# RWKV mixing and a PReLU feed-forward on one core: tiles moved to other addresses, and the last three steps' output products in another order

## The chip, the cores and the metric

One core of a Trainium2 chip runs the whole kernel. The metric is device microseconds of one execution. The kernel before has a median of 498.93 us over three runs (497.51, 498.93, 500.3). One further execution was profiled; everything read from a trace below is from it.

## The reference, cut to what matters

A recurrent mixing layer writes its output `x`, and a feed-forward with a leaky rectifier follows. All is float32.

```
for t in range(768):                       # batch 4, heads 8, head size 48
    cur   = (u * k[t]) outer v[t]
    y[t]  = r[t] @ (state + cur)
    state = w * state + k[t] outer v[t]
x = y as [3072 tokens, 384]
h = x @ w_in                               # 384 x 2048
g = max(h, 0) + alpha * min(h, 0)
out = g @ w_out                            # 2048 x 384
```

## The kernel before, in words

The sequence is cut into 6 chunks of 128 positions. With 4 batches a chunk is 512 tokens. The mixing layer of a chunk is done in a chunked form by small float32 products, in "bursts", one for each of 4 pairs of heads (function `burst`, lines 543 to 605). Their moving operands are slices of 64 columns of `raw` and `base` and of 48 columns of `v`.

The feed-forward (called MoE in the change) takes a chunk in 16 steps of 128 hidden units, 96 steps in all. To keep float32 precision every operand is split into a rounded part and a rest: weights into `wh` and `wl`, the input into `xh` and `xl`, the hidden values into `gh` and `gl`. A product is then three matmuls: high by high, low by high, high by low.

- `m_in(n)`, line 628: nine matmuls of 128x128 weights with 512 moving columns make `h` of one step in one bank of PSUM, three blocks `k` of the contraction by three products. The moving tiles are `xh` and `xl`.
- Then ScalarE copies `h` to `g` (line 636), VectorE makes the rectifier (637), ScalarE rounds it to `gh` (640) and VectorE subtracts to get `gl` (641). `gl` is written by line 641 alone.
- `m_out(n)`, line 661: nine matmuls add the step's share to the three sums `acc0`, `acc1`, `acc2` (one for each block of 128 output rows). The moving tiles are `gh` (six matmuls) and `gl` (three). In every step but the last the order is product by product: `gh` with `wh` into the three sums, `gh` with `wl`, `gl` with `wh`. In the last step it is sum by sum.
- After a chunk's last step ScalarE copies each sum to SBUF (line 688) and a DMA on SyncE's queue stores it (line 690).

`m_out` runs three steps behind `m_in` (`MLAG = 3`), so that the three outer products that are left come one behind the other at the end. The order of all work is planned ahead: each piece has an engine, an estimate of its time, what it reads and writes, and a rank; a list scheduler places a piece as soon as it can begin, the lowest rank first. The result is written out in that order with the scheduling layer in manual mode; that layer adds the semaphore waits from what it sees of tiles and banks.

Tiles have fixed addresses. They are placed one behind the other, each padded to a multiple of 32 bytes. First come the constants and weights (`wh`, `wl`), then the pool `wk`, whose tiles stand in the order in which their names are first used. Small tiles of an odd number of 32-byte units put all that follows off a multiple of 64.

Of the kernel before, what the change touches and what calls it, by code (L numbers as in the profile page):

```python
# [9 lines left out]
F32R = mybir.dt.float32r  # L10
# [14 lines left out]
MLAG = 3  # L25
# [151 lines left out]
def rwkv_prelu_kernel(ctx: ExitStack, tc, rk, vkr, wP, uP, u, wall, alpha, w, r_all, k_all, v_all, oT):  # L177
# [19 lines left out]
    def fixed(shape, name, dt=F32):  # L197
        t = const.tile(shape, dt, name=name)
        return plan.buf(lambda: t)
# [14 lines left out]
    T = [None] * P  # L214

    uw = fixed([112, P, 2], "uw")
    wh, wl = ([fixed([128, 2 * NK, 128], f"{n}{i}", F32R) for i in range(NF)] for n in ("wh", "wl"))
    flag = fixed([1, 1], "flag", I32)

    bank = pb([128, NT], "acc2")  # L220
    plan.banks += [ps.tile([128, NT], F32, name=f"bank{i}") for i in range(5)]
# [256 lines left out]
            cu(), sums()[:, cols].rearrange("p (b g) -> p g b", g=2), AF.Copy), r=[mine], w=[cu], rank=copy_rank)  # L478


    seen_y = fixed([1, 2], "seen_y")
    pairs = [(c, q) for c in range(1, C) for q in range(P)]
    made = {}

# [39 lines left out]
    def burst(i, was, at):  # L524
# [28 lines left out]
        if before:  # L553
            (c0, q0), r0, v0, base0, *states0 = before
            y = [psum() for _ in range(2)]
            uses += [r0, v0, base0, *states0]
            spare = psum()
            writes += y

            def where(g, b, j):  # L560
                o = g ^ (b >> 1)
                return y[g]()[half(o), (b & 1) * L + j * HI:(b & 1) * L + (j + 1) * HI]

            def through_state():
                for j, t in enumerate(states0):
                    for e in range(2):
                        for g in range(2):
                            for b in (e, e + 2):
                                nc.tensor.matmul(where(g, b, j), t()[half(g), b],  # L569
                                                 r0()[half(g), b, HI * j:HI * (j + 1)], start=(j == 0 and e == 0),  # L570
                                                 stop=False, skip_group_check=True)

            def through_scores(crossed):
                for e in (1, 0) if crossed else (0, 1):
                    for g in (1, 0) if crossed else (0, 1):
                        j = g ^ crossed
# [71 lines left out]
    def m_out(n):  # L648
# [11 lines left out]
            for k in ks:  # L660
                nc.tensor.matmul(banks[k](), a[i]()[:, NK + k], x(), start=(begin and j == 0), stop=(end and j == 2))  # L661

        if n == NM - 1:
            for k in range(NK):
                add("PE", 0.7, lambda k=k: [mm(j, (k,)) for j in range(3)], r=[wh[i], wl[i], gh, gl], w=[banks[k]],
                    rank=n + MLAG - 0.5)
        else:
            for j in range(3):
                add("PE", 0.7, lambda j=j: mm(j, range(NK)), r=[wh[i], wl[i], gl if j == 2 else gh], w=banks,
                    rank=n + MLAG - 0.5)  # L670
        if end:
            again = c in seen
            seen.add(c)
            for k in range(NK):
# [19 lines left out]

    def check():

        ok, w2, total = sb([128, NF + P], "ok", 1), sb([112, P], "w2", 1), sb([1, 1], "total", 1)
        count = psum()
        at = 40
        add("POOL", 0.1, lambda: nc.gpsimd.memset(ok(), 0.0), w=[ok], rank=at)  # L700
        add("DVE", 0.1, lambda: nc.vector.tensor_scalar(ok()[:, 0:NF], alph(), 1.0, None, op0=ALU.is_le), r=[alph],
            w=[ok], rank=at)
        add("DVE", 0.1, lambda: nc.vector.tensor_tensor(out=w2(), in0=wp(), in1=wp(), op=ALU.mult), r=[wp], w=[w2],
            rank=at)
        add("DVE", 0.1, lambda: nc.vector.tensor_scalar(ok()[0:112, NF:], w2(), 0.75 ** 2, None, op0=ALU.is_ge),
            r=[w2], w=[ok], rank=at)
        add("DVE", 0.1, lambda: nc.vector.scalar_tensor_tensor(
            out=ok()[0:112, NF:], in0=w2(), scalar=0.75 ** -2, in1=ok()[0:112, NF:], op0=ALU.is_le, op1=ALU.mult),
            r=[w2], w=[ok], rank=at)
        add("PE", 0.3, lambda: nc.tensor.matmul(count()[0:1, 0:NF + P], one()[:, 0:1], ok(), start=True, stop=True), r=[one, ok],  # L710
            w=[count], rank=at)
        add("DVE", 0.1, lambda: nc.vector.tensor_reduce(out=total(), in_=count()[0:1, 0:NF + P], axis=AX.X, op=ALU.add), r=[count],
            w=[total], rank=at)
        add("DVE", 0.1, lambda: nc.vector.tensor_scalar(total(), total(), DFF + 112 * P - 0.5, None, op0=ALU.is_lt),
            w=[total], rank=at)
        add("DVE", 0.1, lambda: nc.vector.tensor_copy(flag(), total()), r=[total], w=[flag], rank=at)


    def warm():
# [180 lines left out]
```

## Time and profile before

| what | value |
|---|---|
| median of three runs | 498.93 us |
| the profiled execution's own time | 498.5 us |
| its span, first to last instruction | 496.7 us |
| TensorE (PE) busy | 477.7 us, 96% |
| VectorE (DVE) busy | 322.1 us, 65% |
| ScalarE (ACT) busy | 242.5 us, 49% |
| DMA, mean over the span | 95 GB/s |

The execution takes 1.8 us more than its span. PE is busy nearly throughout; its matmuls overlap in the records, so that the pace is read from the starts of successive matmuls and from the chain of waits, and not from the busy time of one. A row `L661 PE MATMUL acc<-gl,wh` is a matmul of line 661 that reads `gl` as moving and `wh` as weights and writes a sum.

### The profile page before, as it was taken

The page shows a single profiled execution, that of the slowest core. Times are in us where ns is not written, and L with a number is a line of the kernel's source. Part 1 is how long each engine was busy: PE and PEld are TensorE (multiplying, and loading weights), DVE is VectorE, ACT ScalarE, POOL GpSimd, SP SyncE. Part 2 cuts the span into 40 slices and gives each one's busy share as a digit, 9 for nine tenths or more (in the row PEclk, how much of TensorE's full clock was granted, in tenths as well). Part 3 has the DMA queues.
Part 4 walks back from the last instruction along what each step waited for, and adds up shares of the span by engine and source line. Part 5 has one row for each costly group of instructions (what it writes and reads, how often), then busy time and mean ns, then how long its engine had stood idle before and what let it go on. Part 6 is the DMA issues. An engine that isn't in the chain of part 4 may idle for free.

```text
span 496.7 us, 11103 instructions
## 1 busy us (share of the span) xinstructions
PE 477.7 (96%) x4563; PEld 390.2 (79%) x4563; DVE 322.1 (65%) x550; ACT 242.5 (49%) x565; POOL 45.1 (9%) x49
## 2 busy tenths in 40 slices
PE   7989878999999999999999999999999999999994
PEld 6857756788888888888888888888888878888883
DVE  7799999999986677656647546747535434333331
ACT  3777557666764455535535635535633333423332
POOL 2000100001312112100311101211000000000000
PEclk9799999999999999999999999999999999999998
DMA  7965575374152253413212213312120000100001
GB/s 220 299 172 189 153 226 196 126 233 161 49 189 90 80 169 100 147 43 83 86 36 86 95 56 84 86 36 70 63 54 1 1 1 1 64 0 2 0 1 68
DMA packets 24888, 47.39 MB, mean 95 GB/s; under 512 B 4096, under 2 KB 12416, under 8 KB 24832
## 3 DMA queue, kind: packets, MB, share of 16 engines
q1 hardware_dynamic: 24832, 46.62, 30.3%
q8 instruction: 38, 0.62, 0.5%
q14 instruction: 18, 0.15, 0.1%
HBM read 37.96 MB, written 6.29 MB: 89 GB/s over the span
## 4 chain that ended last, share of the span: by engine, by line
PE 84%; DVE 8%; ACT 3%; DMA 2%; issue 1%; SPq 0%; DVEq 0%; ACTq 0%
PE acc L661 38%; PE bank L628 36%; PE bank L569 2%; PE bank L579 2%; PE bank L550 2%; PE bank L543 2%; DMA wraw<-wall 1%; DVE wx L333 1%; DVE xl L362 1%; DMA raw<-rk 1%; DVE wl L337 1%; DVE wx L330 1%; DVE g L637 1%; PE acc L473 1%; DVE raw L496 1%
## 5 line engine op out<-in xcount | busy, mean ns | idle before, releaser
L637 DVE SCALAR_TENSOR_TENSOR g<-bank,alph,g 128x512 f32<-128x512 f32 x96 | 72.0, 750 | 110.0 <-ACT g L636 108.5
L636 ACT ACTIVATE g<-bank 128x512 f32<-128x512 f32 x96 | 57.3, 597 | 141.0 <-PE bank L628 139.1
L628 PE MATMUL bank<-xh,wh 128*128 128x512 f32 x288 | 113.6, 395 | 3.4 <-DVE T L605 3.4
L628 PE MATMUL bank<-xh,wl 128*128 128x512 f32 x288 | 112.3, 390 | 0.4 <-DVE wl L337 0.3
L628 PE MATMUL bank<-xl,wh 128*128 128x512 f32 x288 | 112.1, 389 | 0.0
L640 ACT ACTIVATE gh<-g 128x512 fp32r<-128x512 f32 x96 | 60.6, 632 | 71.3 <-DVE g L637 71.1
L641 DVE TENSOR_TENSOR gl<-g,gh 128x512 fp32r<-128x512 f32 x96 | 70.0, 730 | 37.1 <-ACT gh L640 37.0
L661 PE MATMUL acc<-gh,wh 128*128 128x512 f32 x288 | 83.6, 397 | 1.6 <-ACT gh L640 1.6
L661 PE MATMUL acc<-gl,wh 128*128 128x512 f32 x288 | 83.2, 396 | 0.0
L661 PE MATMUL acc<-gh,wl 128*128 128x512 f32 x288 | 81.7, 391 | 0.0
L628 PEld LDWEIGHTS bank<-xh,wh 128*128 128x128 f32 x288 | 54.1, 188 | 15.8 <-ACT wx L326 3.8
L628 PEld LDWEIGHTS bank<-xh,wl 128*128 128x128 f32 x288 | 54.1, 188 | 12.6 <-DVE wl L337 1.3
L661 PEld LDWEIGHTS acc<-gl,wh 128*128 128x128 f32 x288 | 54.1, 188 | 12.1
L628 PEld LDWEIGHTS bank<-xl,wh 128*128 128x128 f32 x288 | 54.0, 188 | 11.7
L661 PEld LDWEIGHTS acc<-gh,wl 128*128 128x128 f32 x288 | 53.9, 188 | 11.6
L661 PEld LDWEIGHTS acc<-gh,wh 128*128 128x128 f32 x288 | 52.6, 188 | 13.2 <-ACT gh L640 1.9
L507 POOL TENSOR_TENSOR rr<-rr,kk 128x384 f32<-128x384 f32 x16 | 21.4, 1337 | 294.9 <-DMA kk<-vkr 155.8
L518 ACT ACTIVATE base<-ident,cu 128x64 f32<-128x64 f32 x160 | 41.4, 337 | 1.1 <-DVE cu L513 1.0
L362 DVE TENSOR_TENSOR xl<-bank,xh 48x256 fp32r<-48x256 f32 (+2 forms) x85 | 37.2, 438 | 3.5 <-ACT xh L361 1.7
L361 ACT ACTIVATE xh<-bank 48x256 fp32r<-48x256 f32 (+2 forms) x85 | 33.3, 392 | 7.8 <-PE bank L431 3.4
L496 DVE TENSOR_TENSOR raw<-raw,W 112x512 f32<-112x512 f32 x40 | 26.3, 681 | 0.3 <-DMA raw<-rk 0.3
L509 POOL TENSOR_TENSOR rr<-rr,utab 128x384 f32<-128x384 f32 x16 | 21.0, 1310 | 1.3
(93 smaller groups left out, 375.1 us busy)
## 6 DMA issues: line engine op xcount, KB each, us to landing
wraw<-wall SPq DMA_DIRECT2D x16, 768.0 KB, 4.8
raw<-rk SPq DMA_DIRECT2D x46, 224.0 KB, 4.2
v<-vkr SPq DMA_DIRECT2D x24, 192.0 KB, 4.0
kk<-vkr SPq DMA_DIRECT2D x24, 192.0 KB, 3.6
rr<-vkr SPq DMA_DIRECT2D x16, 192.0 KB, 2.4
oT<-o SPq DMA_DIRECT2D x12, 256.0 KB, 2.1
oT<-g SPq DMA_DIRECT2D x6, 256.0 KB, 2.6
xh<-xh SPq DMA_DIRECT2D x36, 32.0 KB, 2.5
```

Source lines behind the costliest of these rows:

```text
L361: add("ACT", us, lambda: nc.scalar.activation(to(h), view(), AF.Copy), r=[src], w=refs(h), rank=rank)
L362: add("DVE", us + 0.1, lambda: nc.vector.tensor_tensor(out=to(l), in0=view(), in1=to(h), op=ALU.subtract), r=[src] + refs(h), w=refs(l), r ...
L496: add("DVE", 0.72, lambda t=t, tab=tab: nc.vector.tensor_tensor(out=t().rearrange("p b (j t) -> p (b j) t", j=2), in0=t().rearrange("p b ( ...
L507: add("POOL", 1.2, lambda: nc.gpsimd.tensor_tensor(out=rt(), in0=rt(), in1=k(), op=ALU.mult), r=[k] + ([wh[12]] if c == 2 else []), w=[rt] ...
L509: add("POOL", 1.2, lambda: nc.gpsimd.tensor_tensor(out=rt().rearrange("p (g b) e -> p g b e", g=2), in0=rt().rearrange("p (g b) e -> p g b ...
L518: add("ACT", 0.32, lambda g=g, b=b: nc.scalar.activation(base()[:, g, b], ident2(), AF.Copy, scale=cu()[:, g, b:b + 1]), r=[cu, ident2], w ...
L628: nc.tensor.matmul(hp()[:, :], a[i]()[:, k], x[c]()[:, k], start=(k == 0 and j == 0), stop=(k == NK - 1 and j == 2))
L636: add("ACT", 0.6, lambda: nc.scalar.activation(g(), hp()[:, :], AF.Copy), r=[hp], w=[g], rank=n - 100)
L637: add("DVE", 0.75, lambda: nc.vector.scalar_tensor_tensor(out=g(), in0=hp()[:, :], scalar=alph()[:, i:i + 1], in1=g(), op0=ALU.mult, op1=A ...
L640: add("ACT", 0.64, lambda: nc.scalar.activation(gh(), g(), AF.Copy), r=[g], w=[gh], rank=n - 100)
L641: add("DVE", 0.73, lambda: nc.vector.tensor_tensor(out=gl(), in0=g(), in1=gh(), op=ALU.subtract), r=[g, gh], w=[gl], rank=n - 99)
L661: nc.tensor.matmul(banks[k](), a[i]()[:, NK + k], x(), start=(begin and j == 0), stop=(end and j == 2))
```

## The change

Three things.

Addresses. `flag` and `seen_y`, 32 bytes each, now stand between `wh` and `wl` in place of behind `wl`; the tile `ok` grows from 80 to 128 bytes a partition, `w2` and `total` to 64. By the addresses in the two built programs, `gl`, `base`, `v`, `o` and `wraw` began 32 bytes past a multiple of 64 before (`gl` at 168864, 170912 and 172960), and begin at multiples of 64 now (168896, 170944, 172992). `xh`, `xl` and `gh` began at multiples of 64 before too; they are 64 bytes further on now, as is `wl`. `raw` and the three work tiles `g` stay where they were.

Order. The outer products of the last three steps (numbers 93, 94, 95) are pieces of one sum each, with ranks that put the first two sums ahead of the third. On PE the last rows stand so; `acc_4946`, `acc_4948` and `acc_4950` are the three sums, and the number behind `wh` or `wl` tells the step's weights (the kernel before first):

```order
2802 L661 MATMUL acc_4946<-gl,wh_95 128x512 [waits DVE_49]
2803 L661 MATMUL acc_4948<-gl,wh_95 128x512
2804 L661 MATMUL acc_4950<-gl,wh_95 128x512
2805 L661 MATMUL acc_4946<-gh,wh_96 128x512 [waits Activation_49]
2806 L661 MATMUL acc_4946<-gh,wl_112 128x512
2807 L661 MATMUL acc_4946<-gl,wh_96 128x512 [waits DVE_49]
2808 L661 MATMUL acc_4948<-gh,wh_96 128x512
2809 L661 MATMUL acc_4948<-gh,wl_112 128x512
2810 L661 MATMUL acc_4948<-gl,wh_96 128x512
2811 L661 MATMUL acc_4950<-gh,wh_96 128x512
2812 L661 MATMUL acc_4950<-gh,wl_112 128x512
2813 L661 MATMUL acc_4950<-gl,wh_96 128x512
```

The changed kernel at the same place of PE:

```order
2802 L660 MATMUL acc_4946<-gh,wh_96 128x512 [waits Activation_49]
2803 L660 MATMUL acc_4946<-gh,wl_114 128x512
2804 L660 MATMUL acc_4946<-gl,wh_96 128x512 [waits DVE_49]
2805 L660 MATMUL acc_4948<-gh,wh_96 128x512
2806 L660 MATMUL acc_4948<-gh,wl_114 128x512
2807 L660 MATMUL acc_4948<-gl,wh_96 128x512
2808 L660 MATMUL acc_4950<-gh,wh_95 128x512
2809 L660 MATMUL acc_4950<-gh,wl_113 128x512
2810 L660 MATMUL acc_4950<-gl,wh_95 128x512
2811 L660 MATMUL acc_4950<-gh,wh_96 128x512
2812 L660 MATMUL acc_4950<-gh,wl_114 128x512
2813 L660 MATMUL acc_4950<-gl,wh_96 128x512
```

The first sum is ready with the 18th of the last 27 matmuls (before with the 21st), the second with the 21st (before the 24th), the third with the 27th as before. The last step's `gl` is first read by the 18th (before by the 21st). Ahead of these 27 matmuls, PE's instructions stand in the same order in both kernels, and so do those of the other engines.

The last copy. The third sum goes to SBUF in two halves of 256 columns: ScalarE the first, VectorE the second. The end of ScalarE's and of VectorE's queue, the kernel before (ScalarE, then VectorE; the last rows ahead of the test of `flag`):

```order
416 L640 ACTIVATE gh<-g 128x512 [waits DVE_49]
417 L688 ACTIVATE o<-acc_4946 128x512 [waits DMAHW4_49,PE_49]
418 L688 ACTIVATE o<-acc_4948 128x512 [waits DMAHW5_49,PE_49]
419 L688 ACTIVATE g<-acc_4950 128x512 [waits PE_49,Activation_49]
...
549 L637 SCALAR_TENSOR_TENSOR g<-bank_115,alph,g 128x512 [waits Activation_49]
550 L641 TENSOR_TENSOR gl<-g,gh 128x512 [waits PE_49,Activation_49]
```

And the changed kernel:

```order
416 L639 ACTIVATE gh<-g 128x512 [waits DVE_49]
417 L694 ACTIVATE o<-acc_4946 128x512 [waits DMAHW4_49,PE_49]
418 L694 ACTIVATE o<-acc_4948 128x512 [waits DMAHW5_49,PE_49]
419 L689 ACTIVATE g<-acc_4950 128x256 [waits PE_49,Activation_49]
...
549 L636 SCALAR_TENSOR_TENSOR g<-bank_116,alph,g 128x512 [waits Activation_49]
550 L640 TENSOR_TENSOR gl<-g,gh 128x512 [waits PE_49,Activation_49]
551 L691 COPY g<-acc_4950 128x256 [waits Activation_49]
```

VectorE's copy waits for a count of ScalarE's semaphore and for none of PE's. The store of the third sum, which waited for ScalarE, waits for VectorE now.

The diff, cut to its core:

```diff
-    wh, wl = ([fixed([128, 2 * NK, 128], f"{n}{i}", F32R) for i in range(NF)] for n in ("wh", "wl"))
-    flag = fixed([1, 1], "flag", I32)
+    wh = [fixed([128, 2 * NK, 128], f"wh{i}", F32R) for i in range(NF)]
+    flag, seen_y = fixed([1, 1], "flag", I32), fixed([1, 2], "seen_y")
+    wl = [fixed([128, 2 * NK, 128], f"wl{i}", F32R) for i in range(NF)]
...
-        if n == NM - 1:
+        if n >= NM - 3:
+
             for k in range(NK):
+                late = n == NM - 1 or k == NK - 1
                 add("PE", 0.7, lambda k=k: [mm(j, (k,)) for j in range(3)], r=[wh[i], wl[i], gh, gl], w=[banks[k]],
-                    rank=n + MLAG - 0.5)
+                    rank=NM + (k == NK - 1) + 0.5 * late + 0.1 * k + 0.01 * (n - NM))
...
+                elif n == NM - 1 and k == NK - 1:
+                    add("ACT", 0.4, lambda o=o, t=banks[k]: nc.scalar.activation(
+                        o()[:, 0:256], t()[:, 0:256], AF.Copy), r=[banks[k]], w=[(o, 0)], rank=n - 90)
+                    add("DVE", 0.4, lambda o=o, t=banks[k]: nc.vector.tensor_copy(
+                        o()[:, 256:512], t()[:, 256:512]), r=[banks[k]], w=[(o, 1)], rank=n - 90)
...
-        ok, w2, total = sb([128, NF + P], "ok", 1), sb([112, P], "w2", 1), sb([1, 1], "total", 1)
+        ok, w2, total = sb([128, 32], "ok", 1), sb([112, 16], "w2", 1), sb([1, 16], "total", 1)
```

The rest of the diff slices `ok`, `w2` and `total` to their old shapes where they are used, and takes out a name `spare` that nothing used.

## Rows read from the trace of the kernel before

**Rows 1.** Busy time of the engines in stretches of the span: stretch and its length, then PE, PE's weight loads, DVE, ACT, POOL, each with a count of instructions, the granted clock of PE, the share and rate of DMA.

```profile
50.00:100.00 50.00, 43.74 (x600) 34.81 (x599) 48.85 (x82) 30.63 (x67) 2.92 (x2) 0.97 0.57 175
100.00:150.00 50.00, 50.00 (x397) 40.95 (x396) 46.37 (x74) 33.87 (x77) 8.26 (x6) 1.00 0.48 155
...
400.00:450.00 50.00, 50.00 (x278) 40.65 (x277) 19.01 (x28) 17.90 (x32) 0.00 (x0) 1.00 0.05 17
```

**Rows 2.** The chain of waits that ended last, in order of time: start, length, what. A piece of the early part, and the end.

```profile
87.24 0.95 DVE wx L333
...
89.53 0.88 DVE wl L337
...
90.45 4.17 PE bank L628 x17
94.62 2.06 PE acc L661 x9
```

**Rows 3.** The same chain, six steps from the end of the span to the last matmul and the copy behind it.

```profile
461.32 2.04 PE bank L628 x9
463.36 2.06 PE acc L661 x9
...
481.85 2.04 PE bank L628 x9
483.90 6.22 PE acc L661 x27
...
490.20 0.60 ACT g L688
```

**Rows 4.** PE's instructions in order of time in the first and the last of these steps: start, length of the record, what, count.

```profile
461.15 0.40 PE L628 MATMUL bank<-xh,wh 128*128 128x512 f32 x1
461.39 0.39 PE L628 MATMUL bank<-xh,wl 128*128 128x512 f32 x1
...
463.20 0.84 PE L661 MATMUL acc<-gh,wh 128*128 128x512 f32 x3
463.88 0.84 PE L661 MATMUL acc<-gh,wl 128*128 128x512 f32 x3
464.56 0.86 PE L661 MATMUL acc<-gl,wh 128*128 128x512 f32 x3
465.26 0.40 PE L628 MATMUL bank<-xh,wh 128*128 128x512 f32 x1
...
481.69 0.40 PE L628 MATMUL bank<-xh,wh 128*128 128x512 f32 x1
...
483.73 0.84 PE L661 MATMUL acc<-gh,wh 128*128 128x512 f32 x3
```

**Rows 5.** Line 661 from 130 us to the end: the shortest, median and longest record in ns, by what is read.

```profile
L661 PE MATMUL acc<-gl,wh x243: 388/397/397, 130.0 to 489.7; 128*128 128x512 f32 x122
L661 PE MATMUL acc<-gh,wl x241: 387/389/504, 129.8 to 489.5; 128*128 128x512 f32 x121
```

**Rows 6.** PE in the last step, which goes sum by sum: the first and the last of its nine matmuls.

```profile
487.86 0.40 PE L661 MATMUL acc<-gh,wh 128*128 128x512 f32 x1
...
489.71 0.40 PE L661 MATMUL acc<-gl,wh 128*128 128x512 f32 x1
```

**Rows 7.** Instructions that read or write `gl` in two stretches: the columns of rows 1 without POOL, then the clock and DMA.

```profile
0.00:90.00 90.00, 8.46 (x53) 6.23 (x53) 7.58 (x11) 4.99 (x16) 0.94 0.70 210
90.00:490.00 400.00, 77.23 (x268) 50.12 (x267) 65.26 (x89) 0.00 (x0) 1.00 0.22 69
```

**Rows 8.** A burst of the mixing layer on PE, in order of time: 32 matmuls with 64 columns of `raw`, 16 with 64 columns of `base`, then 16 with 48 columns of `v` among others.

```profile
371.05 0.66 PE L569 MATMUL bank<-raw,T 48*48 48x64 f32 x32
371.53 0.41 PE L579 MATMUL bank<-base,v 64*48 64x64 f32 x16
371.75 0.56 PE L543 MATMUL bank<-v,kk 64*64 64x48 f32 x15
372.10 0.27 PE L550 MATMUL bank<-raw 48*64 48x64 f32 x3
```

**Rows 9.** The last step's way from `h` to `gl`, ACT and DVE in order of time.

```profile
483.99 0.60 ACT L636 ACTIVATE g<-bank 128x512 f32<-128x512 f32 x1 [2.06 <-PE bank L628]
484.62 0.75 DVE L637 SCALAR_TENSOR_TENSOR g<-bank,alph,g 128x512 f32<-128x512 f32 x1 [1.96 <-ACT g L636]
485.41 0.63 ACT L640 ACTIVATE gh<-g 128x512 fp32r<-128x512 f32 x1 [0.82 <-DVE g L637]
486.07 0.69 DVE L641 TENSOR_TENSOR gl<-g,gh 128x512 fp32r<-128x512 f32 x1 [0.70 <-ACT gh L640]
```

**Rows 10.** The end, in order of time: copies of the sums on ACT, issues of the stores on SyncE's queue (SPq).

```profile
488.75 1.30 ACT L688 ACTIVATE o<-acc 128x512 f32<-128x512 f32 x2 [2.71 <-PE acc L661]
...
489.38 1.03 SPq L690 DMA_DIRECT2D oT<-o  x2
...
490.82 0.33 SPq L690 DMA_DIRECT2D oT<-g  x1
```

**Rows 11.** Stretches of half a microsecond behind the last matmul, columns as in rows 1.

```profile
490.00:490.50 0.50, 0.10 (x1) 0.00 (x0) 0.00 (x0) 0.35 (x2) 0.00 (x0) 1.00 0.57 217
...
492.00:492.50 0.50, 0.00 (x0) 0.00 (x0) 0.00 (x0) 0.00 (x0) 0.00 (x0) 1.00 0.76 270
492.50:493.00 0.50, 0.00 (x0) 0.00 (x0) 0.00 (x0) 0.00 (x0) 0.00 (x0) 1.00 0.04 16
```

**Rows 12.** Groups by line, the first two over the whole span, the others from 100 to 485 us: count, total busy time and mean ns of one. Copies from PSUM near the size of a half, and the matmuls that read `base`.

```profile
L688 ACT ACTIVATE g<-acc 128x512 f32<-128x512 f32 x4 | 2.4, 601 | 0.2 <-PE acc L661 0.2
L299 DVE COPY whalf<-bank 128x384 f32<-128x384 f32 x1 | 0.6, 559 | 0.2 <-PE bank L296 0.2
...
L361 ACT ACTIVATE xh<-bank 48x256 fp32r<-48x256 f32 x64 | 24.3, 380 | 2.1 <-PE bank L579 1.0
L579 PE MATMUL bank<-base,v 64*48 64x64 f32 x512 | 13.8, 216 | 0.0
L598 DVE COPY_PREDICATED base<-strict,bank 128x256 f32<-128x256 uint8 x32 | 12.5, 444 | 4.1 <-PE bank L550 4.1
```

More of the change, by code (lines that the diff above doesn't have):

```diff
@@ L478, in diagonal @@
             cu(), sums()[:, cols].rearrange("p (b g) -> p g b", g=2), AF.Copy), r=[mine], w=[cu], rank=copy_rank)
-    seen_y = fixed([1, 2], "seen_y")
     pairs = [(c, q) for c in range(1, C) for q in range(P)]
@@ L556, in burst @@
             uses += [r0, v0, base0, *states0]
-            spare = psum()
             writes += y
@@ L702, in check @@
             w=[ok], rank=at)
-        add("DVE", 0.1, lambda: nc.vector.tensor_tensor(out=w2(), in0=wp(), in1=wp(), op=ALU.mult), r=[wp], w=[w2],
+        add("DVE", 0.1, lambda: nc.vector.tensor_tensor(out=w2()[:, 0:P], in0=wp(), in1=wp(), op=ALU.mult), r=[wp], w=[w2],
             rank=at)
-        add("DVE", 0.1, lambda: nc.vector.tensor_scalar(ok()[0:112, NF:], w2(), 0.75 ** 2, None, op0=ALU.is_ge),
+        add("DVE", 0.1, lambda: nc.vector.tensor_scalar(ok()[0:112, NF:NF + P], w2()[:, 0:P], 0.75 ** 2, None, op0=ALU.is_ge),
             r=[w2], w=[ok], rank=at)
         add("DVE", 0.1, lambda: nc.vector.scalar_tensor_tensor(
-            out=ok()[0:112, NF:], in0=w2(), scalar=0.75 ** -2, in1=ok()[0:112, NF:], op0=ALU.is_le, op1=ALU.mult),
+            out=ok()[0:112, NF:NF + P], in0=w2()[:, 0:P], scalar=0.75 ** -2, in1=ok()[0:112, NF:NF + P], op0=ALU.is_le, op1=ALU.mult),
             r=[w2], w=[ok], rank=at)
-        add("PE", 0.3, lambda: nc.tensor.matmul(count()[0:1, 0:NF + P], one()[:, 0:1], ok(), start=True, stop=True), r=[one, ok],
+        add("PE", 0.3, lambda: nc.tensor.matmul(count()[0:1, 0:NF + P], one()[:, 0:1], ok()[:, 0:NF + P], start=True, stop=True), r=[one, ok],
             w=[count], rank=at)
-        add("DVE", 0.1, lambda: nc.vector.tensor_reduce(out=total(), in_=count()[0:1, 0:NF + P], axis=AX.X, op=ALU.add), r=[count],
+        add("DVE", 0.1, lambda: nc.vector.tensor_reduce(out=total()[:, 0:1], in_=count()[0:1, 0:NF + P], axis=AX.X, op=ALU.add), r=[count],
             w=[total], rank=at)
-        add("DVE", 0.1, lambda: nc.vector.tensor_scalar(total(), total(), DFF + 112 * P - 0.5, None, op0=ALU.is_lt),
+        add("DVE", 0.1, lambda: nc.vector.tensor_scalar(total()[:, 0:1], total()[:, 0:1], DFF + 112 * P - 0.5, None, op0=ALU.is_lt),
             w=[total], rank=at)
-        add("DVE", 0.1, lambda: nc.vector.tensor_copy(flag(), total()), r=[total], w=[flag], rank=at)
+        add("DVE", 0.1, lambda: nc.vector.tensor_copy(flag(), total()[:, 0:1]), r=[total], w=[flag], rank=at)
     def warm():
```

## The prediction

> **What bounds the kernel now.** I read the busy times by stretch first. From 100 us on PE is busy without a gap at a granted clock of 1.00, while DVE falls to 19 of 50 us at the end [rows 1]; in the stretch ahead of that DVE is busy 48.85 of 50 us and PE 43.74, so DVE sets the pace there. The chain of waits says the same. Up to 90.45 us it goes over DVE's preparation of weights, and from there over `m_in` and `m_out` of PE without another engine between them [rows 2, 3]. What a matmul costs more or less counts in full behind 90 us and hardly before.
>
> Inside a step, starts are what matters. From the first matmul of `m_in` to the same one five steps later it is 481.69 - 461.15 = 20.54 us, 4.108 for 18 matmuls, or 228.2 ns each [rows 4]. The six with `gh` take 464.56 - 463.20 = 1.36 us, 226.7 each. The eight of `m_in` behind its first take 463.20 - 461.39 = 1.81, 226.3 each. The three with `gl` take 465.26 - 464.56 = 0.70, 233.3 each, and the one behind them, the first of `m_in`, 0.24 and 0.23. So four matmuls in a step are slower than the other fourteen: the three that read `gl` and the one that comes after. The medians of the records say it too: 397 ns with `gl` and 389 with `gh` [rows 5]. At 226.7 for all, a step would take 4.080 us; it takes 0.028 more.
>
> The last step tells whether it is the place in a step or the tile. There `gl` comes third in each group of three. Eight pitches take 489.71 - 487.86 = 1.85 us, 0.036 above eight times 226.7 [rows 6]. Two of these pitches begin with `gl` and three follow one, five times 7 ns is 0.035. The extra goes with `gl`, and stays on the matmul behind it, whatever bank it writes. `gh` and `gl` meet the same weights. What sets `gl` apart is its start 32 bytes past a multiple of 64, where `gh`, `xh` and `xl` all start at one.
>
> **Part 1, addresses.** `gl` starts at a multiple of 64 now, and by this reading its three matmuls and the one behind them come down to 226.7. The saving is 0.027 us a step (between the 0.020 that the three alone show and the 0.028 of the whole step, nearer the second because the last step shows the one behind as well). `gl` is written 89 times behind 90 us and 268 matmul records read it there, 89 steps; the seven before stand in DVE's stretch and save nothing [rows 7]. 89 x 0.027 = 2.4 us, with ends of 1.8 and 2.5.
>
> The other tiles that move: `base` and `v` are moving operands of the bursts. 32 matmuls with `raw`, which starts at a multiple of 64 before and after, take 0.48 us, 15.0 ns each; 16 with `base`, off by 32 bytes, take 0.22, 13.8 each [rows 8]. No cost of the start is to be seen there, so I take nothing. With `v` 15 records take 0.35 us, 23 ns for 48 columns (a few other records are mixed in). If a pitch like that of `base` came out for its 16, 0.15 us in each of 16 bursts (512 matmuls with `base` from 100 to 485 us at 32 a burst [rows 12]), that would be 2.4 us; I take 0, since `base` with the same offset pays nothing, and keep 0.8 as an end, a third of it, as the rows are mixed. `wl`, `xh`, `xl` and `gh` move by 64 bytes and start at multiples of 64 as before: 0. `o` and `wraw` are read by ACT, DVE and DMA beside PE: 0, covered by PE's unbroken work, and in the DVE stretch there is no row that tells one offset from another.
>
> Here a rule speaks against the change. The Trainium skill ("SBUF — State Buffer", section Specifications) gives the lines of SBUF as 16 bytes, with a penalty for each crossing to a new line. A start 32 bytes on is a start of such a line as well, and by that alone `gl` would gain nothing. The trace's 397 against 389 ns does not fit it, unless something else than the start makes `gl` slow; no row shows what a line is.
>
> **Part 2, the order of the last 27 matmuls.** It neither adds nor removes a matmul, and the third sum ends with the 27th as before. The last step's `gh` is wanted by the 16th matmul and its `gl` by the 18th. PE begins the 27 at 483.73 [rows 4]; the 16th starts 15 x 0.227 = 3.40 us later, at 487.13, the 18th at 487.58. `gh` is ready at 485.41 + 0.63 = 486.04 and `gl` at 486.07 + 0.69 = 486.76 [rows 9]. There is 0.8 us in hand: no wait. Matmuls that follow each other into one bank keep their pace in `m_in` (226.3): 0. The first two sums are ready three matmuls, 0.7 us, earlier, and so are their two copies and stores. In the profile, DMA works from about 490.2 to 492.4 without a gap on all three stores [rows 11]; 768 KB in 2.2 us is 0.73 us each. The third store was issued at 490.82; the first, issued at 489.38 [rows 10], began to move data 0.8 us later, so the third would begin at 491.65 and end at 492.4 with nothing ahead of it. It was not held up, or at most by little: I take 0, with ends of 0 and 0.2 saved.
>
> **Part 3, the last copy in halves.** VectorE's half waits for ScalarE's semaphore and for none of PE's, although it reads a bank that PE has only just finished (the rows of the order above). The wait that stands for both can only be that for ScalarE's half copy itself. So the halves go one behind the other. ScalarE takes 601 ns for 512 columns and 380 for 256 [rows 12]. VectorE's nearest rows are 444 ns for a predicated copy of 256 columns and 559 for a plain one of 384; 0.42 for 256 lies between them by proportion of length. A hand from ACT to DVE costs 484.62 - (483.99 + 0.60) = 0.03 us [rows 9]. 0.38 + 0.03 + 0.42 = 0.83 against 0.60: 0.23 us later. The ends are 0.30 later (if both cost what the rows of 256 columns show, with a little for the hand) and 0.18 sooner (0.42 against 0.60, if they ran side by side after all). All that comes behind waits for it: the issue, the store, the end. Nothing covers it.
>
> **Sum.** -2.4 + 0 + 0.23 = -2.2 us. The profiled execution took 498.5 us, 1.8 more than its span of 496.7: 496.3. The median of the runs, 498.93, is 0.4 higher and gives 496.7. I forecast 496.5.
>
> **Rivals.**
> 1. The start address has nothing to do with it (`gl` is slow because DVE writes it, or because of where it stands in the core's memory). Then Part 1 is 0, Part 3 stays: 498.93 + 0.23 = 499.2, slower. The place is the last copy, the price 0.23 us, and it decides as soon as the saving is under 0.23 / 89 = 2.6 ns a step. For it: the trace holds no run of `gl` at another address, and the skill's rule above comes out here, with this time. Against it: `xl` is written by DVE too and its matmuls take the 226.3 of `m_in`, and the extra follows `gl` through two different orders. 12%.
> 2. The change doesn't do what it says, in its favour: the halves do run side by side, or the stores gain from the free queue. Then the end is 0.2 to 0.4 sooner in place of 0.23 later: 496.1 or so. The missing wait on PE speaks against it. 5%.
> 3. `v`, too, pays for its start now: another 0.8 us off, 495.8. For it the 23 ns in rows 8, against it `base` in the same rows. 8%.
> 4. The pace of 226.7 is itself a cost of the start: `xh`, `xl` and `gh` stood 64 bytes past a multiple of 128 and stand at one now. If that were worth another 7 ns on 14 matmuls a step, 89 x 14 x 0.007 = 8.7 us would go: 487.8. Against it: `gl` stood 32 bytes past a multiple of 128, nearer to it, and was slower; two points cannot exclude it. 3%.
>
> My forecast has the rest, 72%, with a range of its own of 495.8 to 497.5: the ends of Part 1 (0.6 up, 0.1 down) and of Part 3, and the spread of the runs shown, which lie 1.4 us to either side of their median. The range for 8 in 10 is 495.0 to 498.3: it takes in rivals 2 and 3, and leaves out rival 4 and most of rival 1.
>
> A measurement of this kernel can tell about 0.5%, 2.5 us, from no change. My forecast is 0.45 to 0.5% below before, just inside. Faster by more than that needs all of Part 1 and a bit from rival 2, 3 or 4, or luck of the runs: a third of my forecast's chance, 24%, and 10% from those rivals, 34% in all. Slower by more than 0.5% has no mechanism here, 2%. The rest, 64%, is no change.
>
> **What would show it.** Right: with `gl` and with `gh` the same median record, 389; the three `gl` and the one behind at 226.7; a step of 4.08 us; no PE wait in the last 27 matmuls; ACT's half copy near 0.38, DVE's behind it and not beside it, the last issue 0.23 us later after the last matmul's end than the 490.82 of before. Wrong: a step still at 4.108 (rival 1), a DVE copy that starts with ACT's (rival 2), a shorter burst (rival 3), all matmuls under 226 (rival 4).

## The result, and the profile after

The changed kernel took 504.28 us (median of 9 runs, 503.32 to 505.82), the kernel before 499.76 beside it (9 runs, 497.51 to 502.35). The recorded ratio of the runs is 1.0082 with a 95% interval of 1.006 to 1.0104 (the two medians alone give 1.0090): 3.0 to 5.2 us slower, where 2.2 us less were forecast. 504.28 lies outside the range of 495.0 to 498.3.

Profiled was an execution of 504.54 us, with a span of 502.8 where before had 496.7. The chain of waits of the changed kernel, in order of time (start, length, what), answers to [rows 2] and [rows 3]; `m_in` stands at L627 now, `m_out` at L660:

```profile
91.87 4.20 PE bank L627 x17
...
365.60 2.09 PE bank L627 x9
367.69 2.09 PE acc L660 x9
...
373.95 2.09 PE bank L627 x9
...
442.29 2.07 PE bank L627 x9
444.36 2.08 PE acc L660 x9
...
487.90 2.07 PE bank L627 x9
489.97 6.26 PE acc L660 x27
...
```

Nine matmuls of `m_in` took 2.04 us before and take 2.07 to 2.09; nine of `m_out` took 2.06 and take 2.08 to 2.09. Eleven steps, 442.29 to 487.90, last 45.61 us, 4.146 each; the two from 365.60 to 373.95 last 4.175 each. Before it was 4.107, and 4.080 was forecast. So the same tiles run at two paces in one execution: the nines of the chain mostly take 2.09 and 2.09 us up to the last burst, at 413.74, and 2.07 and 2.08 behind it.

The span grew by 6.1 us, and the chain says where:

- Until PE's unbroken part begins: 90.45 to 91.87, 1.4 us. That start moves about from kernel to kernel in the experiments below, from 89.94 (e4) to 95.42 (e1), and e1's operands all lie where they lay before. I don't put it down to the change.
- From there to the last 27 matmuls, the "unbroken part": 483.90 - 90.45 = 393.45 before, 489.97 - 91.87 = 398.10 after. 4.65 us more, on PE alone, at a granted clock of 1.00 in both kernels from 100 us to 485. This is about the whole of the 4.5 us between the medians.
- The last 27: 6.22 and 6.26.
- From the last matmul's start to the last store's issue: 490.82 - 489.71 = 1.11 before, 497.18 - 495.83 = 1.35 after, 0.24 more. From the issue to the end of the span: 5.9 and 5.6.

Which matmuls got slower is seen in the records of PE from 130 us to the end (shortest, median and longest in ns, the first and last start, shape and count), to be read against [rows 5]:

```profile
L627 PE MATMUL bank<-xl,wh x236: 392/397/398, 129.6 to 489.6; 128*128 128x512 f32 x118
L627 PE MATMUL bank<-xh,wh x235: 389/392/504, 129.9 to 489.1; 128*128 128x512 f32 x118
...
L660 PE MATMUL acc<-gh,wl x243: 387/395/497, 131.3 to 495.6; 128*128 128x512 f32 x122
...
L660 PE MATMUL acc<-gl,wh x243: 388/393/398, 132.0 to 495.8; 128*128 128x512 f32 x122
```

The median with `gl` did come down, from 397 to 393. But those with `gh`, `xh` and `xl`, which were to stay, are at 392 to 397, where [rows 5] has 389 with `gh`. All six products pay, 18 matmuls in a step instead of four. The change in the record of one matmul is small; what counts is the pitch, the time from one matmul's start to the next one's. The weight loads have a median of 187 to 188 ns. No wait of PE stands in the unbroken part.

The end, in order of time; in brackets the idle time before an instruction and what ended it. It answers to [rows 10]:

```profile
495.83 0.39 PE L660 MATMUL acc<-gl,wh 128*128 128x512 f32 x1
496.31 0.38 ACT L689 ACTIVATE g<-acc 128x256 f32<-128x256 f32 x1 [0.85 <-PE acc L660]
496.73 0.42 DVE L691 COPY g<-acc 128x256 f32<-128x256 f32 x1 [3.89 <-ACT g L689]
497.18 0.33 SPq L696 DMA_DIRECT2D oT<-g  x1
```

The two halves go one behind the other, 0.38 and 0.42 us, as forecast.

### The profile page after: what moved, and what is told of

Read it like the earlier page. It is cut to its first block, busy times and chain, and to the rows that moved or that the text cites. A ratio compares the mean times of both kernels' runs of the same rounds, so it can differ in the third digit from the quotient of the medians.

```text
span 502.8 us, 11104 instructions
## 1 busy us (share of the span) xinstructions
PE 482.9 (96%) x4563; PEld 390.8 (78%) x4563; DVE 325.8 (65%) x551; ACT 242.2 (48%) x565; POOL 41.7 (8%) x49
## 4 chain that ended last, share of the span: by engine, by line
PE 83%; DVE 6%; DMA 5%; ACT 2%; issue 2%; SPq 1%; ACTq 0%; DVEq 0%
PE acc L660 38%; PE bank L627 38%; DMA wraw<-wall 3%; PE bank L568 2%; PE bank L578 2%; PE bank L550 2%; PE bank L543 1%; DMA o<-rk 1%; DVE wx L334 1%; DVE wx L331 1%; DMA kk<-vkr 1%; DVE xl L363 1%; DVE wl L338 1%; DVE raw L496 1%; SPq L376 1%
## 5 line engine op out<-in xcount | busy, mean ns | idle before, releaser
L627 PE MATMUL bank<-xh,wh 128*128 128x512 f32 x288 | 115.8, 402 | 4.4 <-DVE T L604 3.4
L627 PE MATMUL bank<-xl,wh 128*128 128x512 f32 x288 | 115.4, 401 | 0.0
L627 PE MATMUL bank<-xh,wl 128*128 128x512 f32 x288 | 114.6, 398 | 0.1
L660 PE MATMUL acc<-gh,wh 128*128 128x512 f32 x288 | 85.3, 401 | 2.1 <-ACT gh L639 2.1
L660 PE MATMUL acc<-gh,wl 128*128 128x512 f32 x288 | 83.9, 396 | 0.0
L660 PE MATMUL acc<-gl,wh 128*128 128x512 f32 x288 | 83.2, 393 | 0.0
L627 PEld LDWEIGHTS bank<-xh,wh 128*128 128x128 f32 x288 | 55.3, 192 | 17.9 <-ACT wx L327 3.8
L627 PEld LDWEIGHTS bank<-xh,wl 128*128 128x128 f32 x288 | 55.3, 192 | 13.2 <-DVE wl L338 0.5
L627 PEld LDWEIGHTS bank<-xl,wh 128*128 128x128 f32 x288 | 54.9, 191 | 12.6
L660 PEld LDWEIGHTS acc<-gh,wl 128*128 128x128 f32 x288 | 54.1, 189 | 12.8
L660 PEld LDWEIGHTS acc<-gh,wh 128*128 128x128 f32 x288 | 52.6, 188 | 14.5 <-ACT gh L639 2.4
L660 PEld LDWEIGHTS acc<-gl,wh 128*128 128x128 f32 x288 | 54.1, 188 | 12.4
L507 POOL TENSOR_TENSOR rr<-rr,kk 128x384 f32<-128x384 f32 x16 | 19.4, 1214 | 302.7 <-DMA kk<-vkr 193.0
L509 POOL TENSOR_TENSOR rr<-rr,utab 128x384 f32<-128x384 f32 x16 | 19.7, 1229 | 1.3
```

Of the source, the lines that this page charges most:

```text
L507: add("POOL", 1.2, lambda: nc.gpsimd.tensor_tensor(out=rt(), in0=rt(), in1=k(), op=ALU.mult), r=[k] + ([wh[12]] if c == 2 else []), w=[rt] ...
L509: add("POOL", 1.2, lambda: nc.gpsimd.tensor_tensor(out=rt().rearrange("p (g b) e -> p g b e", g=2), in0=rt().rearrange("p (g b) e -> p g b ...
L627: nc.tensor.matmul(hp()[:, :], a[i]()[:, k], x[c]()[:, k], start=(k == 0 and j == 0), stop=(k == NK - 1 and j == 2))
```

## The experiments

Where a tile begins in a partition of SBUF can be read from the compiled program. The diff moves more than its text shows: behind `wh` everything shifts by the 64 bytes of `flag` and `seen_y`, and everything made after `check` by the 128 bytes of the padded tiles. The table gives each start modulo 256 (`x` for `xh` and `xl`), with the time. A step is the mean of the steps in the last stretch of PE's chain, behind the last burst, where nothing else runs on PE. "Part" is the unbroken part of the chain, from the row of 17 matmuls between 89 and 96 us to the last 27.

| kernel | `wh` | `wl` | `x` | `gh` | `gl` | step, us | part, us | ratio to before (95%) |
|---|---|---|---|---|---|---|---|---|
| before | 192 | 192 | 192 | 192 | 160 | 4.107 | 393.45 | 1 |
| changed | 192 | 0 | 0 | 0 | 192 | 4.146 | 398.10 | 1.0082 (1.006 to 1.0104) |
| e1_tail_only | 192 | 192 | 192 | 192 | 160 | 4.107 | 393.41 | 1.0004 (0.9969 to 1.0039) |
| e2_addr_only | 192 | 0 | 0 | 0 | 192 | 4.147 | 398.06 | 1.009 (1.0058 to 1.0121) |
| e3_wl_only | 192 | 0 | 192 | 192 | 160 | 4.173 | 398.58 | 1.0103 (1.007 to 1.0136) |
| e4_pool_only | 192 | 192 | 0 | 0 | 192 | 4.170 | 398.45 | 1.0112 (1.0073 to 1.0151) |
| e5_gl_alone | 192 | 192 | 192 | 192 | 192 | 4.080 | 391.46 | 0.9945 (0.9907 to 0.9983) |
| e6_all_at_0 | 0 | 0 | 0 | 0 | 0 | 4.080 | 391.40 | 0.9959 (0.9927 to 0.9991) |
| e7_all_at_96 | 224 | 224 | 224 | 224 | 224 | 4.080 | 391.43 | 0.9965 (0.9935 to 0.9995) |
| e8_half_256 | 192 | 192 | 64 | 64 | 192 | 4.173 | 398.92 | 1.009 (1.0064 to 1.0116) |
| e9_change_at_192 | 192 | 192 | 192 | 192 | 192 | 4.080 | 391.47 | 0.9959 (0.9928 to 0.9991) |
| e10_order_one_copy | 192 | 192 | 192 | 192 | 192 | 4.080 | 391.44 | 0.9935 (0.991 to 0.996) |
| e11_gl_at_0 | 192 | 192 | 192 | 192 | 0 | 4.153 | 396.98 | 1.0068 (1.0041 to 1.0096) |
| e12_two_tiles | 192 | 192 | 192 | 192 | 192 | 4.080 | 391.42 | 0.9952 (0.9921 to 0.9983) |

The first question was which part of the change costs: the addresses (theory A in the expectations), or the order and the copy at the end (theory B). These two kernels divide it.

**e1_tail_only**: before, with the change's order of the last 27 and its copy in halves, all tiles where they lay.

```diff
-        if n == NM - 1:
+        if n >= NM - 3:
...
+                late = n == NM - 1 or k == NK - 1
...
-                    rank=n + MLAG - 0.5)
+                    rank=NM + (k == NK - 1) + 0.5 * late + 0.1 * k + 0.01 * (n - NM))
...
+                elif n == NM - 1 and k == NK - 1:
+                    add("ACT", 0.4, lambda o=o, t=banks[k]: nc.scalar.activation(
+                        o()[:, 0:256], t()[:, 0:256], AF.Copy), r=[banks[k]], w=[(o, 0)], rank=n - 90)
+                    add("DVE", 0.4, lambda o=o, t=banks[k]: nc.vector.tensor_copy(
+                        o()[:, 256:512], t()[:, 256:512]), r=[banks[k]], w=[(o, 1)], rank=n - 90)
```

> The kernel before with the new order of the last 27 matmuls and the last copy in two halves, all addresses as before. If the loss of 4.5 us lies in the addresses (theory A), this takes 0.1 to 0.3 us more than before, a ratio of 1.000 to 1.001, and a step stays at 4.108 us. If it lies in the new order or the halves (theory B), 1.007 to 1.009.

**e2_addr_only**: the changed kernel without those two edits.

```diff
-        if n >= NM - 3:
+        if n == NM - 1:
...
-                    rank=NM + (k == NK - 1) + 0.5 * late + 0.1 * k + 0.01 * (n - NM))
+                    rank=n + MLAG - 0.5)
...
-                elif n == NM - 1 and k == NK - 1:
```

> The changed kernel with the old order at its end and the old single copy: only addresses are new. Theory A: 1.006 to 1.010 and a step of 4.15 to 4.18 us as in the changed kernel. Theory B: 0.994 to 1.000.

e1 took 500.85 us beside 500.54 of before, e2 504.73. The chain of e1, columns as above:

```profile
95.42 4.16 PE bank L628 x17
...
484.72 2.06 PE acc L661 x9
486.78 2.04 PE bank L628 x9
488.83 6.25 PE acc L661 x27
```

2.06 and 2.04 as in [rows 3], and 488.83 - 95.42 = 393.41 for the unbroken part against 393.45. So the whole of the loss is with the addresses, though they gave `gl` the start that it was to have. The next two take the two shifts apart.

**e3_wl_only**: before with `flag` and `seen_y` between `wh` and `wl`, which moves `wl` by 64 bytes and no other of the tiles.

```diff
-    wh, wl = ([fixed([128, 2 * NK, 128], f"{n}{i}", F32R) for i in range(NF)] for n in ("wh", "wl"))
-    flag = fixed([1, 1], "flag", I32)
+    wh = [fixed([128, 2 * NK, 128], f"wh{i}", F32R) for i in range(NF)]
+    flag, seen_y = fixed([1, 1], "flag", I32), fixed([1, 2], "seen_y")
+    wl = [fixed([128, 2 * NK, 128], f"wl{i}", F32R) for i in range(NF)]
```

> The kernel before with wl alone moved by 64 bytes, so that wh and wl differ in their place within 128 bytes; no moving tile is moved. If the loss comes from the weights (theory A1, loads of 188 ns become 191 to 192), 1.005 to 1.010 and steps of 4.15 us or more. If it comes from the moving tiles (theory A2), 0.999 to 1.001 and 4.108. If only both together make it (theory A3, their places against each other), something between 1.002 and 1.008.

**e4_pool_only**: before with the change's sizes in `check`, which move the moving operands and no weights.

```diff
-        ok, w2, total = sb([128, NF + P], "ok", 1), sb([112, P], "w2", 1), sb([1, 1], "total", 1)
+        ok, w2, total = sb([128, 32], "ok", 1), sb([112, 16], "w2", 1), sb([1, 16], "total", 1)
```

> The kernel before with the tiles behind the weights at the changed kernel's addresses (gl, base, v, o, wraw by 32 bytes, xh, xl and gh by 64), wl where it was. A1: the gain that was forecast, 0.994 to 0.997, and 4.08 us a step. A2: 1.005 to 1.010 and 4.15 or more. A3: something between, other matmuls slow than with wl moved.

506.25 and 505.35 us: either shift alone costs, and about as much as both together, by the unbroken part 398.58 and 398.45 us against 398.10. (Both ratios lie a little above the 1.010 that was expected at most.) By e3 the weights are at fault, by e4 the moving tiles, so neither is it alone. The chain of e3:

```profile
94.66 4.19 PE bank L628 x17
...
493.24 6.30 PE acc L661 x27
```

In e3, where nothing but `wl` moved, from one multiple of 64 to another, the nine of `m_in` take 2.08 and those of `m_out` 2.09. PE's records behind 130 us show that not only products with `wl` are longer: `gh` with `wh` has 394 ns, and had 389 before. First the row of the kernel before, then those of e3:

```profile
L661 PE MATMUL acc<-gh,wh x240: 389/389/501, 132.8 to 489.3; 128*128 128x512 f32 x120
```

```profile
L661 PE MATMUL acc<-gl,wh x244: 392/394/398, 129.8 to 499.1; 128*128 128x512 f32 x122
L661 PE MATMUL acc<-gh,wh x243: 387/394/497, 133.4 to 498.7; 128*128 128x512 f32 x122
L661 PE MATMUL acc<-gh,wl x243: 388/397/497, 134.0 to 498.9; 128*128 128x512 f32 x122
```

The loads of the weights keep their 188 ns, so the loss isn't a longer load. What e3, e4 and the changed kernel share is that some weights and some moving tiles lie at different places. That made a third theory (C): what counts is that the operands of matmuls which follow each other lie at the same place within some length, not whether a tile begins at a multiple of anything. The rivals to it: that the place itself counts (E), or that multiples of 64 are needed as well, as I had read it (F).

**e5_gl_alone**: before, with `gl` moved by 32 bytes, to 192 like the rest, and nothing else (`w2` lies inside `ok` now; the other lines only slice it).

```diff
-        ok, w2, total = sb([128, NF + P], "ok", 1), sb([112, P], "w2", 1), sb([1, 1], "total", 1)
+        ok, total = sb([128, 32], "ok", 1), sb([1, 1], "total", 1)
+        w2 = plan.buf(lambda: ok()[0:112, 24:24 + P])
```

> The kernel before with gl (and o, v, base, wraw) 32 bytes further on, and nothing else moved: w2 lies inside ok. All six operands of the big matmuls then stand 64 past a multiple of 128 (and 192 past one of 256). Theory C (a pitch of 226.7 ns needs weights and moving tiles at the same place within 128 bytes, whichever it is): every matmul at 226.7, a step of 4.08 us, 2.4 us less than before, a ratio of 0.994 to 0.998. Theory D (the starts of gl and of the others have no such common law, gl is slow by itself): 4.107 a step and 0.999 to 1.002.

**e6_all_at_0**: e2 with `flag` and `seen_y` ahead of `wh` and `ok` of 48 columns, `w2` inside: all six operands at a multiple of 256.

```diff
-    wh = [fixed([128, 2 * NK, 128], f"wh{i}", F32R) for i in range(NF)]
     flag, seen_y = fixed([1, 1], "flag", I32), fixed([1, 2], "seen_y")
-    wl = [fixed([128, 2 * NK, 128], f"wl{i}", F32R) for i in range(NF)]
+    wh, wl = ([fixed([128, 2 * NK, 128], f"{n}{i}", F32R) for i in range(NF)] for n in ("wh", "wl"))
...
+        ok, total = sb([128, 48], "ok", 1), sb([1, 1], "total", 1)
```

> Weights wh and wl, xh, xl, gh and gl all at multiples of 256 bytes. Theory C: 226.7 for every matmul, 4.08 a step, 0.994 to 0.998. Theory E (each tile by itself: 64 past a multiple of 128 is fast, a multiple of 128 slow): all matmuls at 231 or more, 4.15 to 4.2 a step, 1.005 to 1.012.

**e7_all_at_96**: e5 with `flag` ahead of `wh` and `ok` of 40 columns: all six operands at 224, 32 bytes past a multiple of 64, as `gl` was in before.

```diff
-    wh, wl = ([fixed([128, 2 * NK, 128], f"{n}{i}", F32R) for i in range(NF)] for n in ("wh", "wl"))
     flag = fixed([1, 1], "flag", I32)
+    wh, wl = ([fixed([128, 2 * NK, 128], f"{n}{i}", F32R) for i in range(NF)] for n in ("wh", "wl"))
...
-        ok, total = sb([128, 32], "ok", 1), sb([1, 1], "total", 1)
+        ok, total = sb([128, 40], "ok", 1), sb([1, 1], "total", 1)
```

> All six operands 96 bytes past a multiple of 128, so that none begins at a multiple of 64, and all at the same place. Theory C: 4.08 a step, 0.994 to 0.998. If a start at a multiple of 64 matters by itself (theory F), every matmul costs what gl cost before, 234 ns: 4.21 a step, 1.01 to 1.02.

**e8_half_256**: before with `ok` of 32 and `w2` of 32 columns: `gl` goes to 192 like the weights, `xh`, `xl` and `gh` go on by 128 bytes, to 64. All six operands agree within 128 bytes, not within 256.

```diff
-        ok, w2, total = sb([128, NF + P], "ok", 1), sb([112, P], "w2", 1), sb([1, 1], "total", 1)
+        ok, w2, total = sb([128, 32], "ok", 1), sb([112, 32], "w2", 1), sb([1, 1], "total", 1)
```

> All six operands 64 past a multiple of 128, but xh, xl and gh are 64 past a multiple of 256, and wh, wl and gl 192 past one. Theory C with a length of 128 bytes: 4.08 a step, 0.994 to 0.998. Theory C with a length of 256 bytes: the slow pace of the changed kernel, 4.14 to 4.2 a step, 1.005 to 1.012.

Beside 500.57 of before they took 497.65 (e5), 497.94 (e6), 499.05 (e7) and 504.58 (e8). The chain of e7, whose six operands all lie off every multiple of 64:

```profile
90.13 4.17 PE bank L628 x17
...
477.48 2.04 PE acc L661 x9
479.52 2.04 PE bank L628 x9
481.56 6.13 PE acc L661 x27
```

`m_in` and `m_out` both take 2.04, 9 x 226.7 ns, as in e5 and e6. Its records with `gl`, over all of the span, have the median that `gh` had before:

```profile
L661 PE MATMUL acc<-gl,wh x288: 387/389/397, 42.1 to 487.3; 128*128 128x512 f32 x144
```

So 0, 192 and 224 are equally good places if all six operands share one: neither the place nor a multiple of 64 counts. And the chain of e8, whose `xh`, `xl` and `gh` lie 128 bytes from the other three:

```profile
487.11 2.09 PE acc L661 x9
489.20 2.08 PE bank L628 x9
491.28 6.23 PE acc L661 x27
```

Slow, so agreement within 128 bytes isn't enough; 256 is. (A longer length is out: in before and in e5 the weights lie 256 bytes apart from `xh` and `xl` modulo 512, at 192 against 448, and e5 has the full pace.)

What e5 gives is what Part 1 of the prediction was to give: 483.90 - 90.45 = 393.45 comes down to 484.42 - 92.96 = 391.46, 2.0 us, by its chain:

```profile
92.96 4.15 PE bank L628 x17
...
482.38 2.04 PE bank L628 x9
484.42 6.13 PE acc L661 x27
```

The last four kernels ask whether the change's other parts are worth something with the addresses mended, and test my first reading against the new one once more.

**e9_change_at_192**: the changed kernel with e5's addresses.

```diff
-    wh = [fixed([128, 2 * NK, 128], f"wh{i}", F32R) for i in range(NF)]
-    flag, seen_y = fixed([1, 1], "flag", I32), fixed([1, 2], "seen_y")
-    wl = [fixed([128, 2 * NK, 128], f"wl{i}", F32R) for i in range(NF)]
+    wh, wl = ([fixed([128, 2 * NK, 128], f"{n}{i}", F32R) for i in range(NF)] for n in ("wh", "wl"))
+    flag = fixed([1, 1], "flag", I32)
...
-        ok, w2, total = sb([128, 32], "ok", 1), sb([112, 16], "w2", 1), sb([1, 16], "total", 1)
+        ok, total = sb([128, 32], "ok", 1), sb([1, 1], "total", 1)
+        w2 = plan.buf(lambda: ok()[0:112, 24:24 + P])
```

> The change's new order of the last 27 matmuls and its copy in halves, at the addresses of e5 (all six operands 192 past a multiple of 256). Theory C: 4.080 a step; the last issue of a store stands 0.2 us later behind the last matmul than in before; in all 2 us less than before, a ratio of 0.993 to 0.998. If the order costs more than its halves (theory B), over 0.998.

**e10_order_one_copy**: e9 with the last sum copied whole by ScalarE.

```diff
-                elif n == NM - 1 and k == NK - 1:
-                    add("ACT", 0.4, lambda o=o, t=banks[k]: nc.scalar.activation(
...
-                    add("DVE", 0.4, lambda o=o, t=banks[k]: nc.vector.tensor_copy(
...
```

> As e9, with the third sum copied whole by ScalarE again. Theory C: 0.2 us less than e9, a ratio of 0.993 to 0.998 (the difference to e9 is too small for the times and is read in the profile: from the last matmul's end to the end of the span as in before, or up to 0.2 us less if the third store gains from the two earlier ones).

**e11_gl_at_0**: before, with `gl` moved from 160 to 0, a multiple of 256; the others stay at 192.

```diff
-        ok, w2, total = sb([128, NF + P], "ok", 1), sb([112, P], "w2", 1), sb([1, 1], "total", 1)
+        ok, w2, total = sb([128, 48], "ok", 1), sb([112, 48], "w2", 1), sb([1, 1], "total", 1)
```

> The kernel before with gl at a multiple of 256, so of 64 too, and the five other operands 192 past a multiple of 256 as before (xh, xl and gh 256 bytes further on). My prediction's reading (gl is slow because it is off a multiple of 64): 4.080 a step, 0.994 to 0.998. Theory C with 256 bytes (gl is slow because it is off the others' place): the matmuls with gl at 232 or more and a step of 4.10 us or more, 0.999 to 1.006.

**e12_two_tiles**: e9 with VectorE's half in a tile of its own, each half with its own store.

```diff
+                    o2 = sb([128, NT], "gl", 3)
...
+                    for x, cols in ((o, slice(0, 256)), (o2, slice(256, 512))):
+                        add("SP", 0.45, lambda k=k, x=x, cols=cols: nc.sync.dma_start(
...
```

> As e9, with the two halves of the third sum in two tiles with a store of their own each. VectorE still waits for ScalarE, since both read one bank. If the first half's store runs beside the second half's copy, the end of the last store is 0.1 to 0.4 us sooner than in e9; if an issue more costs as much, no sooner. In the times as e9 and e10, 0.993 to 0.998.

Beside 500.24 of before they took 498.69 (e9), 498.17 (e10), 504.0 (e11) and 498.14 (e12). PE in e11, in order of time:

```profile
464.10 0.84 PE L661 MATMUL acc<-gh,wl 128*128 128x512 f32 x3
464.78 0.87 PE L661 MATMUL acc<-gl,wh 128*128 128x512 f32 x3
465.48 0.40 PE L628 MATMUL bank<-xh,wh 128*128 128x512 f32 x1
...
467.57 0.85 PE L661 MATMUL acc<-gh,wh 128*128 128x512 f32 x3
468.25 0.84 PE L661 MATMUL acc<-gh,wl 128*128 128x512 f32 x3
468.93 0.87 PE L661 MATMUL acc<-gl,wh 128*128 128x512 f32 x3
```

By my first reading `gl` has the best of starts here and should cost nothing; by the new one it is the tile that stands out. It stands out: its three take 465.48 - 464.78 = 0.70 us. The nine of `m_in` behind it take 467.57 - 465.48 = 2.09, 232 ns each, although `wh`, `wl`, `xh` and `xl` agree. The six with `gh` are back at 226.7 (468.93 - 467.57 = 1.36). So one tile that is off slows matmuls that don't read it. (The ratio of e11, 1.0068, lies just above the 0.999 to 1.006 that theory C gave.)

One rival to C has no kernel of its own: that the two weights must agree with each other, and the four moving tiles with each other, but not the one kind with the other. In every slow kernel an operand differs from others of its own kind too. What speaks for C is e8 beside e11. In both the weights agree and one moving tile, `gl`, lies apart from the other three. In e11 those three lie with the weights, and the six with `gh` take 1.36 us; in e8 they don't, and the six take 471.65 - 470.25 = 1.40:

```profile
470.25 0.85 PE L661 MATMUL acc<-gh,wh 128*128 128x512 f32 x3
...
471.65 0.85 PE L661 MATMUL acc<-gl,wh 128*128 128x512 f32 x3
```

That is an argument and not a proof, as `gl` also lies farther off in e8, 128 bytes against 64.

The end of e9, columns as for the changed kernel, and that of e10:

```profile
489.48 0.39 PE L661 MATMUL acc<-gl,wh 128*128 128x512 f32 x1
...
490.38 0.42 DVE L692 COPY g<-acc 128x256 f32<-128x256 f32 x1 [3.76 <-ACT g L690]
490.83 0.33 SPq L697 DMA_DIRECT2D oT<-g  x1
```

```profile
492.12 0.39 PE L661 MATMUL acc<-gl,wh 128*128 128x512 f32 x1
492.61 0.60 ACT L690 ACTIVATE g<-acc 128x512 f32<-128x512 f32 x1 [0.82 <-PE acc L661]
493.23 0.33 SPq L692 DMA_DIRECT2D oT<-g  x1
```

1.35 us from the last matmul's start to the issue with halves, 1.11 without. In e12 the DVE half still waits for the ACT half, though it writes another tile, so what they share is the bank that they read. (The Trainium skill, "PSUM — Partial Sum Buffer", section PSUM bank collisions raise a hardware error, says that two engines must not be in one bank and the same partitions at once, two reads included, and that the compiler back end's scheduler adds a dependency between two such instructions; the trace agrees in so far as the copies go one behind the other, 0.38 and then 0.42 us. No run here shows two such reads at once.) Its first store goes out 0.90 us behind the last matmul's start, its second 1.35:

```profile
489.83 0.39 PE L661 MATMUL acc<-gl,wh 128*128 128x512 f32 x1
...
490.73 0.42 DVE L693 COPY gl<-acc 128x256 f32<-128x256 f32 x1 [3.76 <-ACT g L691]
490.73 0.33 SPq L696 DMA_DIRECT2D oT<-g  x1
491.18 0.37 SPq L696 DMA_DIRECT2D oT<-gl  x1
```

The times of e5, e9, e10 and e12 don't tell these ends apart: their intervals overlap. Nor does the end of the span: from the last matmul's start to it there are 7.7 us in e9, 7.4 in e10 and 7.1 in e12, but 7.1 in e5 and 5.4 in e8, which both end as before does. So whether a second store brings the end forward, as the expectation for e12 allowed, stays open. All four beat both kernels; e10 has the lowest ratio, 0.9935, and e5 the smallest edit.

## Why the prediction was wrong, point by point

- **What bounds the kernel**: right. The 4.65 us are all on PE behind 90 us, at full count, with no engine in between.
- **Part 1, `gl`**: the reading that the extra goes with the tile and not with its turn was right, and so was its size: 2.4 us forecast, with an end of 1.8, and 2.0 in e5's unbroken part, with 0.09 more in the last 27 (6.22 to 6.13). The reason was wrong. I wrote that what sets `gl` apart is "its start 32 bytes past a multiple of 64". e7 has all six operands there and runs at 226.7 ns; e11 has `gl` at a multiple of 256 and is slower than before. `gl` was slow because it lay elsewhere than the others. In before the other five operands lay at 192, and one odd tile shows only that it differs, not from what.
- **The step that failed**: "`wl`, `xh`, `xl` and `gh` move by 64 bytes and start at multiples of 64 as before: 0." The change put them at 0 while `wh` stayed at 192 and `gl` came to 192. In place of 0 it cost 398.10 - 391.46 = 6.6 us against e5, where all lie alike: 4.146 to 4.175 us a step instead of 4.080, on all six products. e3 shows it for `wl` alone (1.0103), e4 for the moving tiles alone (1.0112). The trace of before held a warning that I used only once: every operand of full pace lay at the same place, so it had no row for two multiples of 64 that disagree. A case that a trace doesn't show can still be given a bound, and the slow rows at hand gave the price: 7 ns, as with `gl`, on 18 matmuls instead of four, 89 x 14 x 0.007 = 8.7 us. I had this sum in rival 4, with the other sign.
- **`base` and `v`**: right at 0. A burst of the changed kernel on PE, in order of time, takes 0.48, 0.23 and 0.34 us from start to start, [rows 8] 0.48, 0.22 and 0.35. Rival 3 didn't happen.

```profile
375.97 0.66 PE L568 MATMUL bank<-raw,T 48*48 48x64 f32 x32
376.45 0.41 PE L578 MATMUL bank<-base,v 64*48 64x64 f32 x16
376.68 0.56 PE L543 MATMUL bank<-v,kk 64*64 64x48 f32 x15
377.02 0.27 PE L550 MATMUL bank<-raw 48*64 48x64 f32 x3
```

- **Part 2, the order**: right, at 0. No wait of PE behind 92 us; the 27 took 6.26 us, and in e1, at the addresses of before, 6.25 against 6.22.
- **Part 3, the halves**: right at the issue, 0.24 us later where 0.23 was forecast. At the end of the span it can't be seen: from the last matmul's start to the end it is 496.7 - 489.71 = 7.0 before and 502.8 - 495.83 = 7.0 after. From the last issue to the end, profiled executions with one copy differ by more than 0.24 (497.3 - 491.26 = 6.0 in e5, 502.3 - 496.62 = 5.7 in e2), so whether the 0.24 us reaches the end stays open.
- **Rivals and chances**: none held the case that came. Rival 1 (the start counts for nothing) would have given 4.107. Rival 4 was nearest in kind, a place within a longer block, with the gain where the loss was. "Slower by more than 0.5% has no mechanism here, 2%" was the wrong sentence to rest on: a start that moves from a known place to one that the trace doesn't show is a mechanism.
- **The Trainium skill's rule** ("SBUF — State Buffer", section Specifications: 16-byte lines, a penalty for each crossing to a new line): I weighed it for `gl` alone. Since 32 and 64 are multiples of 16, by that rule alone no such shift costs anything. That doesn't agree with e3, where 64 bytes of `wl` made 4.107 us a step into 4.173; the measurement decides.

Open stays why a shared place within 256 bytes matters, and why `gl` off by 32 bytes costs 0.027 us a step and off by 64 (e11) 4.153 - 4.080 = 0.073. No run tells where in the chip weights and moving tiles meet, nor why a burst can leave the changed kernel at another pace.

## What to carry to other kernels

Where PE runs large float32 matmuls like these one behind the other (128x128 weights loaded for each, 512 columns), let all operands, weights and moving tiles alike, begin at the same place modulo 256 bytes; 0, 192 and 224 did equally well. Other shapes weren't tried, but for the bursts' small matmuls, which took the same before and after the change. A small tile made early shifts all that come after it, so list the starts of the tiles before and after such an edit. If one tile of a trace is slow, ask what it differs from, not only what it is: try it with that tile alone moved (e5) before everything else moves with it. Two engines that copy halves of one bank went one behind the other here, 0.38 + 0.42 us against 0.60 for one.

## What was not expected of the hardware

- The pace of a matmul depends on how its operands lie to those of its neighbours: 226.7 ns where all lie alike; where they don't, 230 to 232 on average over a step in the slow kernels (4.146 to 4.173 us for 18), and 232 also on matmuls whose own tiles agree (e11).
- The places don't add up. By the last stretch `wl` alone costs 4.173 - 4.107 = 0.066 us a step, the moving tiles alone (with `gl` mended) 0.063, both together 0.039; but up to the last burst both together mostly run at 4.17 as well, and over the unbroken part the three cost 5.1, 5.0 and 4.65 us more than before.
- In e4 a step takes by turns 4.14 and 4.20 us (its chain has nines of 2.10, 2.10, 2.07, 2.07), with the same tiles in each; what alternates wasn't found.
- The weight loads keep medians of 187 to 189 ns throughout: the place is paid for in the pitch of the matmuls, and a load's own record is no longer.
